# Strassen's block products for the second half of the last matrix product, in a kernel of attention, routed experts and a dense layer

## The chip, the core and the metric

The kernel runs on one core of a Trainium2 chip. The metric is device time in microseconds (us), from start to end of one execution. Smaller is better.

The core has a matrix engine (TensorE, PE in the profile; PEld is its loading of stationary weights), an elementwise engine (VectorE, DVE), an engine for functions and copies (ScalarE, ACT), GpSimd (POOL) and SyncE (SP), which here issues the transfers. Each engine works through its own list of instructions in order and waits on semaphores of the others.

## The reference, cut to what matters

```python
attn = softmax(mask(q @ k.T / 8))          # 4 x 8 heads, 576 positions, window of 64
x    = (attn @ v) as 2304 tokens x 512
logits = x @ phi                           # 8 experts x 4 slots
slot_out[e] = relu(slot_input[e] @ w1[e]) @ w2[e]
x = softmax(logits, over slots) @ slot_out
h = x @ w_in                               # 2304 x 512 by 512 x 2048
g = max(h, 0) + log1p(exp(-abs(h)))        # softplus
out = g @ w_out                            # 2304 x 2048 by 2048 x 512, float32
```

The change is in the last line. `w_in` and `w_out` arrive as 64-bit floats, and the kernel turns them into 32-bit ones itself.

## The kernel before, in words

Attention, routing and experts end at about 126.6 us of the trace. The change touches nothing ahead of that; what follows is the last phase.

**Units and groups.** The 2048 inner columns are 16 units of 128, the 2304 tokens 18 tiles of 128, in five groups (`GROUPS`) of 4, 4, 4, 3 and 3 tiles. For a group and a unit there is one item: TensorE makes `h` with the inner columns on the partitions (`do_h`, L933), ScalarE takes the softplus into `g` (`do_g`, L937).

**Split in two.** The matrix engine's fast 32-bit type keeps fewer digits than a float. So each operand is split: `gh` is `g` rounded to that type (`do_gh`, a cast at L838 on ScalarE or VectorE), `gl` is the rest `g - gh` (`do_gl`, L841 on VectorE); `w_out` is split likewise (tile `whl`, steps SH and SL). The product of a tile and a unit (step Y, `do_y`) is three matmuls into one PSUM bank of 512 columns: gh by high (L958), gh by low (L959), gl by high (L960). 18 tiles by 16 units by 3 are 864 of them.

**Turns.** `SLABS` cuts each group's units in three turns, since the weights arrive and are converted slowly (four elementwise steps for each of 32 chunks, `conv`, three of them on VectorE alone). A turn that ends leaves its sum in `part` (`do_o`: a copy after the first turn, an addition on VectorE after the second, L969; after the third an addition into `o` and the store, L975 and L976). One tile of the last group is taken in two halves of 256 columns in its last turn, so that its end comes sooner.

**Order.** Nothing is scheduled on the chip. `arrange` is a planner in the program that builds the kernel: from steps with assumed costs, dependences and due times it makes one list per engine. `TWEAKS` shifts due times by seeded random numbers. What it writes is a static order.

Of the kernel before, what the change touches and what calls it, by code (L numbers as in the profile page):

```python
# [44 lines left out]
DELAY = dict(E=0.2, Q=1.0)  # L45
# [87 lines left out]
def block_kernel(ctx: ExitStack, tc: tile.TileContext, qk, v, phi, w1, w2, w_in, w_out, out):
# [468 lines left out]
    with tc.manual_schedule():  # L602
# [168 lines left out]


        def conv(dst, src):
# [41 lines left out]
        parts_of = {2: (1,), 3: (2, 3), 4: (4, 5), 5: (6, 7)}  # L815

        def width(n):
            return 256 * len(parts_of[n])

        start = [sum(GROUPS[:g]) for g in range(len(GROUPS))]  # L820
        items = []
        for n in range(len(SLABS[0]) - 1):
            for g, nt in enumerate(GROUPS):
                a, b = SLABS[g][n:n + 2]
                for f in range(a, b):
                    cut = (0, 1, nt) if g == 0 and f == 0 else (0, nt)
                    items += [(g, f, f == a, f == b - 1, x, y) for x, y in zip(cut, cut[1:])]
        part, hl, st, y_t = {}, {}, {}, {}
# [133 lines left out]
        def do_o(e, i, j):
            g, f = items[i][:2]
            y, *more = y_t.pop((g, j))
            if f == SLABS[g][1] - 1:
                copy(e, part[g, j], y)
                return
            if f < 15:
                nc.vector.tensor_tensor(out=part[g, j], in0=y, in1=part[g, j], op=ALU.add)  # L969
                return  # L970
            ot = gp.tile([128, 512], F32, tag="o", name="o", bufs=3)
            t = start[g] + j
            for h, y in enumerate((y, *more)):
                c = slice(y.shape[1] * h, y.shape[1] * h + y.shape[1])
                nc.vector.tensor_tensor(out=ot[:, c], in0=y, in1=part[g, j][:, c], op=ALU.add)  # L975
                nc.sync.dma_start(out=out[128 * t:128 * t + 128, c], in_=ot[:, c])  # L976

        def do_r(e, *r):
# [12 lines left out]
        for h in range(2):
            step(("SO", h), dict(D=0.35), rel=L2_END + 0.42 * h - 0.3)
            step(("ST", h), dict(E=0.43), [("SO", h)])
            step(("SE", h), dict(A=0.26, D=0.33), [("ST", h)])
        for n, r in enumerate(raws):
            kind, j, u = r
            rest = [("C",) + raws[x] + (3,) for x in (n - 2 * NB, n - 2 * NB + 1) if n % 2 == 0 and x >= 0]
            step(("R",) + r, dict(Q=1.4), [("R",) + raws[n - 1]] + rest, rel=0.0 if n < NEARLY else 0.1 + 1.4 * NEARLY + 2.55 * NLAST)
            deps = [("R",) + r]
            if n:  # L1000
                deps.append(("C",) + raws[n - 1] + (0,))
            if n > 2:
                deps.append(("C",) + raws[n - 3] + (3,))
            deps += ([] if j < 3 else [("WD", 0, 1), ("WD", 1, 1)] if j == 3 else [("WA", (j - 3) // 2 + 2)]) if kind == "wi" else [("SL", 2 * j - 4 + u)]
            for k in range(4):
                costs = dict(D=0.335, A=0.62, P=1.0) if k == 0 else dict(D=(0.335, 0.6, 0.6)[k - 1])
                step(("C",) + r + (k,), costs, deps if k == 0 else [("C",) + r + (k - 1,)])
            if kind == "wo":
                m = 2 * j + u
                step(("SH", m), dict(A=0.58, D=0.42), [("C", "wo", j, u, 3), ("SH", m - 1)])  # L1010
                step(("SL", m), dict(P=1.25, D=0.69) if m < 2 else dict(D=0.69), [("SH", m)])
            elif j == 0:
                for h in range(2):
                    step(("WD", u, h), dict(E=0.45), [("C", "wi", 0, u, 3), ("SE", h), ("WD", u, h - 1)])
                step(("PC", u), dict(A=0.25, D=0.28), [("WD", u, 1)])
                step(("PS", u), dict(D=0.3), [("PC", u)])
            elif u == 1 and j % 2:
                n = (j + 3) // 2
                w = width(n) // 256
                step(("WA", n), dict(E=0.19 + 0.43 * w), [("C", "wi", x, y, 3) for x in parts_of[n] for y in range(2)] + [("PS", n - 1)])  # L1020
                step(("WQ", n), dict(A=0.26, D=0.33) if w == 1 else dict(A=0.59, D=0.69), [("WA", n), ("WB", n - 1)])
                step(("WL", n), dict(D=0.4 if w == 1 else 0.69), [("WQ", n)])
                step(("WB", n), dict(E=0.26 if w == 1 else 0.5), [("WL", n)])
# [77 lines left out]
```

## Time and profile before

| | |
|---|---|
| median of 3 runs | 361.4 us (361.08 to 362.69) |
| the profiled execution, its span from the first to the last instruction | 361.2 us |
| TensorE busy | 350.2 us (97%) |
| VectorE busy | 234.5 us (65%) |
| ScalarE busy | 155.6 us (43%) |
| last phase, 126.6 us to the end | 234.6 us |

The profiled execution is known by its span; 0.2 us lie between it and the median of the runs. Matmuls are pipelined: a record of one is longer than the distance to the next, and the distance from start to start is what one costs. The same holds for VectorE in a row of instructions that wait for nothing.

### The profile page before, as it was taken

To read this page: it belongs to the slowest core of one execution; us is meant where nothing else is said; L and a number is where in the kernel's file an instruction comes from. 1 tells how busy PE (TensorE), PEld (TensorE's weight loads), DVE (VectorE), ACT (ScalarE), POOL (GpSimd) and SP (SyncE) were. 2 spreads that over 40 slices of the span, in tenths; PEclk is the share of its full clock that TensorE was granted. 3 is DMA by queue.
4 is the path that set the end of the run, shared out by engine and by line. 5 is a ranking of instruction groups with operands and counts; after the bars stand their busy time and mean duration, and the time that the engine had idled before them with its cause. 6 is when DMAs were issued, how large, how long until landed. Compare 5 with 4: busy or idle time off the path is not lost.

```text
span 361.2 us, 7741 instructions
## 1 busy us (share of the span) xinstructions
PE 350.2 (97%) x2996; PEld 266.6 (74%) x2996; DVE 234.5 (65%) x717; ACT 155.6 (43%) x309; POOL 65.3 (18%) x93
## 2 busy tenths in 40 slices
PE   8999998999999999999999999999999999999995
PEld 6788776877434277877888878878888888888884
DVE  4677676874642299998999999954254263354632
ACT  1676665765410089876233656443034122122220
POOL 3997766771040000000000000000000000000000
PEclk9999999999999999999999999999999999999999
DMA  7999999999999964553053341000030020011102
GB/s 283 412 410 405 408 411 386 406 408 397 392 419 419 409 236 142 206 210 141 21 213 116 116 177 58 1 2 0 0 118 0 0 87 31 0 58 60 70 18 88
DMA packets 18180, 69.84 MB, mean 193 GB/s; under 512 B 2016, under 2 KB 2400, under 8 KB 14304
## 3 DMA queue, kind: packets, MB, share of 16 engines
q1 hardware_dynamic: 18000, 69.09, 49.1%
q8 instruction: 23, 0.38, 0.4%
q10 hardware_dynamic: 144, 0.26, 0.2%
q14 instruction: 13, 0.11, 0.1%
HBM read 64.63 MB, written 4.72 MB: 192 GB/s over the span
## 4 chain that ended last, share of the span: by engine, by line
PE 81%; DMA 13%; issue 1%; DVE 1%; POOL 1%; ACT 1%; SPq 0%; DVEq 0%; POOLq 0%; ACTq 0%
PE y_ps L959 19%; PE y_ps L958 19%; PE y_ps L960 18%; DMA w2t<-w_d 6%; PE x_ps L322 5%; DMA raw<-w_out_d 5%; PE pt_ps L304 5%; PE h_ps L933 5%; PE s_ps L277 4%; PE xt_ps L345 2%; DMA v_three<-v_d 2%; PE lt_ps L355 1%; PE wq_ps L900 1%; PE sl_ps L398 1%; POOL sm L295 1%
## 5 line engine op out<-in xcount | busy, mean ns | idle before, releaser
L959 PE MATMUL y_ps<-whl,gh 128*128 128x512 f32 (+1 forms) x295 | 115.6, 392 | 0.0
L958 PE MATMUL y_ps<-whl,gh 128*128 128x512 f32 (+1 forms) x295 | 114.9, 390 | 0.0
L960 PE MATMUL y_ps<-whl,gl 128*128 128x512 f32 (+1 forms) x295 | 114.5, 388 | 0.0
L937 ACT ACTIVATE g<-h_ps 128x512 f32<-128x512 f32 (+2 forms) x81 | 43.6, 553 | 105.7 <-PE h_ps L933 99.1
L958 PEld LDWEIGHTS y_ps<-whl,gh 128*128 128x128 f32 x295 | 55.4, 188 | 15.1 <-issue 2.5
L960 PEld LDWEIGHTS y_ps<-whl,gl 128*128 128x128 f32 x295 | 55.4, 188 | 12.4
L959 PEld LDWEIGHTS y_ps<-whl,gh 128*128 128x128 f32 x295 | 55.4, 188 | 11.4
L841 DVE TENSOR_TENSOR gl<-g,gh 128x512 fp32r<-128x512 f32 (+2 forms) x81 | 50.1, 628 | 3.8 <-ACT gh L838 1.6
L838 DVE CAST gh<-g 128x512 fp32r<-128x512 f32 (+1 forms) x48 | 19.1, 401 | 48.1 <-ACT g L937 47.3
L288 DVE CUSTOM_DVE_ANT_0 sm<-s_ps,cst_sb 128x128 f32<-128x128 f32 x144 | 32.1, 287 | 12.2 <-PE s_ps L277 11.5
L295 POOL TENSOR_TENSOR sm<-mx,sm 128x512 f32<-128x512 f32 x36 | 36.6, 1039 | 7.0 <-DVE mx L288 6.1
L933 PE MATMUL h_ps<-cT,wst 128*128 128x512 f32 (+2 forms) x81 | 28.4, 375 | 0.2 <-DVE wst L841 0.2
L298 ACT ACTIVATE sm<-sm 128x512 f32<-128x512 f32 x36 | 22.4, 635 | 12.0 <-POOL sm L295 11.9
L242 ACT COPY pt<-pt_ps 128x512 f32<-128x512 f32 x36 | 19.6, 588 | 11.8 <-PE pt_ps L304 11.6
L277 PE MATMUL s_ps<-qkb 64*64 64x128 f32 x576 | 21.3, 281 | 1.0 <-issue 0.9
L789 DVE SCALAR_TENSOR_TENSOR cv<-raw,cv 128x512 int32<-128x512 int32 x32 | 21.4, 686 | 0.1
L322 PE MATMUL x_ps<-vd,pt 128*64 128x65 f32 x288 | 21.1, 225 | 0.2
L975 DVE TENSOR_TENSOR o<-y_ps,part 128x512 f32<-128x512 f32 (+1 forms) x19 | 12.3, 661 | 13.3 <-PE y_ps L960 13.1
L322 PEld LDWEIGHTS x_ps<-vd,pt 128*64 128x64 f32 x288 | 18.4, 137 | 3.5 <-issue 2.5
L304 PE MATMUL pt_ps<-cst_sb,sm 128*128 128x128 f32 x144 | 19.7, 278 | 0.5 <-ACT sm L298 0.5
L838 ACT CAST gh<-g 128x512 fp32r<-128x512 f32 (+1 forms) x32 | 18.3, 573 | 3.5 <-PE y_ps L959 2.9
L277 PEld LDWEIGHTS s_ps<-qkb 64*64 64x64 f32 x576 | 16.5, 136 | 4.1 <-issue 3.6
(151 smaller groups left out, 413.0 us busy)
## 6 DMA issues: line engine op xcount, KB each, us to landing
w1t<-w_d SPq DMA_DIRECT2D x15, 1024.0 KB, 10.8
w2t<-w_d SPq DMA_DIRECT2D x13, 1024.0 KB, 11.5
qkb<-qk_d SPq DMA_DIRECT2D x17, 512.0 KB, 9.1
raw<-w_in_d SPq DMA_DIRECT2D x16, 512.0 KB, 4.1
raw<-w_out_d SPq DMA_DIRECT2D x16, 512.0 KB, 4.2
out_d<-o SPq DMA_DIRECT2D x17, 256.0 KB, 2.0
v_three<-v_d SPq DMA_DIRECT2D x10, 260.0 KB, 8.4
vt<-v_d SPq DMA_DIRECT2D x8, 260.0 KB, 8.5
```

The lines of the kernel that those rows point to most:

```text
L277: nc.tensor.matmul(s_ps[2 * t + a][64 * par:64 * par + 64, 128 * p:128 * p + 128], qkb[rows, b, 0, p, 64 * par:64 * par + 64], rhs, start= ...
L288: nc.vector.tensor_tensor_reduce(out=sm[:, p], in0=ps[:, 128 * p:128 * p + 128], in1=mask, scale=-0.125, scalar=3.0e38, op0=ALU.add, op1=A ...
L295: nc.gpsimd.tensor_tensor(out=sm_t[i], in0=mb, in1=sm_t[i], op=ALU.subtract)
L304: nc.tensor.transpose(ps[:, 128 * p:128 * p + 128], sm[:, p], ident)
L322: nc.tensor.matmul(x_ps[64 * par:64 * par + 64, a, 65 * p:65 * p + 65], pt[:, 128 * p + 64 * par:128 * p + 64 * par + 64], vt[:, 65 * h:65 ...
L838: (nc.scalar.copy if e == "A" else nc.vector.tensor_copy)(dst, src)
L841: eng[e].tensor_tensor(out=dst, in0=a, in1=b.bitcast(F32), op=ALU.subtract)
L933: nc.tensor.matmul(st["h", i], wst[:, 128 * f:128 * f + 128], cT[:, o:o + ncol(i)], start=True, stop=True)
L937: nc.scalar.activation(out=st["g", i], in_=st["h", i], func=AF.Softplus)
L958: nc.tensor.matmul(y, st["gh", i][:, ts], hi[:, c], start=first, stop=False)
L959: nc.tensor.matmul(y, st["gh", i][:, ts], lo[:, c], start=False, stop=False)
L960: nc.tensor.matmul(y, st["gl", i][:, ts], hi[:, c], start=False, stop=last)
```

## The change

Units 0 to 7 stay as they were, in two turns instead of three (`SLABS` has three numbers for a group). Groups are now 4, 4, 4, 4 and 2 tiles. Units 8 to 15 are taken in four pairs: for a group and a pair, `g` is a 2 by 2 matrix of blocks (two halves of the tokens by two units), and `w_out` one of two units by two halves of 256 columns. Strassen's method makes the 2 by 2 block product from seven block products in place of eight, each of a sum or difference of blocks. So:

- the sums of weights (steps TA, TB, TC into `txs`; TH, TL, TK, TM split them) are made once for each pair;
- the sums of tokens (XA, XB, XC, then HX, LX, HG, LG split them) are made for each group and pair, 20 times;
- each of the seven products (P, `do_p`) is three matmuls of 256 columns for every tile of half a group, summed over the four pairs in a PSUM bank of its own (banks 0 to 6; `h` uses bank 7);
- after the last pair each of the seven sums is copied out by ScalarE (MC, not in the last group) and added to or taken from up to four blocks of `part` by VectorE (M, `do_m`), which is stored from there.

The rounding casts `gh` and of the new splits stand on ScalarE alone. `TWEAKS` (47 entries) is replaced by another list (27 entries); with that and new costs the whole last phase has a new static order.

```diff
-GROUPS = (4, 4, 4, 3, 3)
-SLABS = ((0, 1, 5, 16), (0, 1, 6, 16), (0, 2, 7, 16), (0, 3, 8, 16), (0, 4, 9, 16))
+GROUPS = (4, 4, 4, 4, 2)
+NN = 8
+SLABS = ((0, 1, NN), (0, 2, NN), (0, 3, NN), (0, 4, NN), (0, 4, NN))
...
-ENGINES = dict(GL="D", GH="AD", SH="AD", SL="PD", WQ="AD", PC="A", O="AD", CE="AD", SO="D", SE="AD", C="AD")
+ENGINES = dict(GL="D", GH="A", SH="A", SL="PD", WQ="AD", PC="A", O="A", CE="AD", SO="D", SE="AD", C="AD", TH="A", TK="A", HX="A", HG="A")
...
-DELAY = dict(E=0.2, Q=1.0)
+DELAY = dict(E=0.2, Q=1.0, D=0.19, A=0.22)
...
+PRODUCTS = ((2, 5, 3), (3, 6, 2), (4, 0, 6), (5, 1, 5), (6, 4, 4), (0, 3, 1), (1, 2, 0))
...
+        def do_ta(e, j):
+            w = wt["pair", j]
+            eng[e].tensor_tensor(out=halves_of(txs[:, 0:512]), in0=two(w[:, 0:256], 512, 256), in1=two(w[:, 256:512], 512, 256), op=ALU.add)
...
+        def do_tl(e, j):
+            h, l = t_tiles(j)
+            sub(e, l[:, 0:1280], txs, h[:, 0:1280])
...
-            for h, y in enumerate(y_t[g, j]):
-                c = slice(y.shape[1] * h, y.shape[1] * h + y.shape[1])
-                nc.tensor.matmul(y, st["gh", i][:, ts], hi[:, c], start=first, stop=False)
-                nc.tensor.matmul(y, st["gh", i][:, ts], lo[:, c], start=False, stop=False)
-                nc.tensor.matmul(y, st["gl", i][:, ts], hi[:, c], start=False, stop=last)
+            nc.tensor.matmul(y, st["gh", i][:, ts], hi, start=first, stop=False)
+            nc.tensor.matmul(y, st["gh", i][:, ts], lo, start=False, stop=False)
+            nc.tensor.matmul(y, st["gl", i][:, ts], hi, start=False, stop=last)
...
+        def do_xa(e, s):
+            w, b = tokens(s), gbuf[s]
+            eng[e].tensor_tensor(out=xbuf(s)[:, 0:2 * w], in0=b[:, 0:2 * w], in1=b[:, 2 * w:4 * w], op=ALU.add)
+
+        def do_xb(e, s):
+            w, b = tokens(s), gbuf[s]
+            eng[e].tensor_tensor(out=halves_of(xbuf(s)[:, 2 * w:4 * w]), in0=halves_of(b[:, w:3 * w]), in1=two(b[:, 0:w], 3 * w, w), op=ALU.subtract)
...
+        def do_hx(e, s):
+            w = tokens(s)
+            copy(e, s_tile(s, 0)[:, 0:5 * w], xbuf(s)[:, 0:5 * w])
+
+        def do_lx(e, s):
+            w = tokens(s)
+            sub(e, s_tile(s, 1)[:, 0:5 * w], xbuf(s)[:, 0:5 * w], s_tile(s, 0)[:, 0:5 * w])
+
+        def do_p(e, s, i):
+            g, p = PAIRS[s]
+            b, x, y = PRODUCTS[i]
...
+            for n, (a, t) in enumerate(((0, hi), (0, lo), (1, hi))):
+                for j in range(nj):
+                    nc.tensor.matmul(
+                        ps[:, 256 * j:256 * j + 256], s_tile(s, a)[:, w * x + 128 * j:w * x + 128 * j + 128], t,
...
+        def do_mc(e, g, i):
+            w = 128 * GROUPS[g]
+            t = gp.tile([128, 512], F32, tag=("gh", "gl")[(7 * g + i) % 2], name="m")
+            nc.scalar.copy(t[:, 0:w], m_ps[g, i][:, 0:w])
...
+            def both(a, c, step, op):
+                x = v[:, a, :, 256 * c:256 * c + 256]
+                o = bass.AP(tensor=x.tensor, offset=x.offset, ap=[list(x.ap[0]), [step, 2], *(list(y) for y in x.ap[1:])])
+                mm = bass.AP(tensor=m.tensor, offset=m.offset, ap=[list(m.ap[0]), [0, 2], *(list(y) for y in m.ap[1:])])
+                nc.vector.tensor_tensor(out=o, in0=o, in1=mm, op=op)
...
+            if k == 5:
+                both(0, 1, 512 * nj, ALU.subtract)
+            elif k == 6:
+                both(0, 0, 512 * nj, ALU.add)
+            elif k == 0:
+                put(0, 1, ALU.add)
+                put(0, 0, ALU.subtract)
...
+            elif k == 3:
+                put(0, 0, ALU.add)
+                store(0)
```

**Place 1, TensorE at the start of the last phase, before.** `so_ps` and `wp_ps` turn the slots' outputs and `w_in` into the weights of `h`, `c_ps` transposes the routing weights, `warm_ps` is work without use.

```order
L855 MATMUL so_ps<-cst_sb,wit 128x128 x4
L889 MATMUL wp_ps<-wit,part 128x128 x4
L733 MATMUL c_ps<-identr,cc 128x128 x8
...
L889 MATMUL wp_ps<-wit,part 128x128 x2
L933 MATMUL h_ps<-cT,wst 128x512
L958 MATMUL y_ps<-whl,gh 128x512
L959 MATMUL y_ps<-whl,gh 128x512
L960 MATMUL y_ps<-whl,gl 128x512
L889 MATMUL wp_ps<-wit,part 128x128 x2
```

The same place now.

```order
L1032 MATMUL so_ps<-cst_sb,wit 128x128 x4
L1100 MATMUL wp_ps<-wit,part 128x128 x4
L919 MATMUL c_ps<-identr,cc 128x128 x12
...
L1144 MATMUL h_ps<-cT,wst 128x512
L1100 MATMUL wp_ps<-wit,part 128x128 x4
L1168 MATMUL y_ps<-whl,gh 128x512
L1169 MATMUL y_ps<-whl,gh 128x512
L1170 MATMUL y_ps<-whl,gl 128x512
```

All four `wp_ps` of the second unit now stand ahead of the first Y; two of them stood behind it.

**Place 2, VectorE in the second half of the last phase, before.** The casts and rests of `g`, and the final additions.

```order
L838 CAST gh<-g 128x512
L841 TENSOR_TENSOR gl<-g,gh 128x512
L975 TENSOR_TENSOR o<-y_ps,part 128x512
L838 CAST gh<-g 128x512
L841 TENSOR_TENSOR gl<-g,gh 128x512
L975 TENSOR_TENSOR o<-y_ps,part 128x512 x2
```

The same place now, one pair of a four-tile group and what stands between. `txs` and `cvx` hold the sums of tokens of alternate pairs, `shl` the split ones, `m` a copied product sum.

```order
L1213 TENSOR_TENSOR txs<-g_3548 128x512
L1217 TENSOR_TENSOR txs<-g_3548 128x512
L1221 TENSOR_TENSOR txs<-g_3548 128x256
L1273 TENSOR_TENSOR part<-part,m 128x4x256
L1012 TENSOR_TENSOR shl<-g_3548,shl 128x512
L1012 TENSOR_TENSOR shl<-txs,shl 128x1280
L1213 TENSOR_TENSOR cvx<-g_3599 128x512
L1221 TENSOR_TENSOR cvx<-g_3599 128x256
L1217 TENSOR_TENSOR cvx<-g_3599 128x512
L1273 TENSOR_TENSOR part<-part,m 128x4x256
```

The casts are gone from VectorE; sums of tokens, their rests and the additions of the block products have come.

**Place 3, VectorE at the very end, before.**

```order
L841 TENSOR_TENSOR gl<-g,gh 128x384 x2
L975 TENSOR_TENSOR o<-y_ps,part 128x512 x2
L975 TENSOR_TENSOR o<-y_ps,part 128x256 x2
```

And now (the 640 columns are the last pair's sums of tokens).

```order
L1012 TENSOR_TENSOR shl<-g_4481,shl 128x256
L1267 TENSOR_TENSOR part<-part,m 128x2x256
L1012 TENSOR_TENSOR shl<-cvx,shl 128x640
L1273 TENSOR_TENSOR part<-part,m_ps 128x2x256 x2
L1267 TENSOR_TENSOR part<-part,m_ps 128x256 x2
L1273 TENSOR_TENSOR part<-part,m_ps 128x2x256
L1267 TENSOR_TENSOR part<-part,m_ps 128x256 x4
```

Behind the last rest of tokens stand nine additions of the last group, where four final additions stood.

## Rows read from the trace of the kernel before

**Rows 1.** The page: busy time, share and instructions; busy tenths in 40 slices.
```profile
PE 350.2 (97%) x2996; PEld 266.6 (74%) x2996; DVE 234.5 (65%) x717; ACT 155.6 (43%) x309; POOL 65.3 (18%) x93
...
DVE  4677676874642299998999999954254263354632
```
**Rows 2.** Busy time by stretch: length, PE, PEld, DVE, ACT, POOL, clock, DMA.
```profile
126.60:132.60 6.00, 5.47 (x39) 4.70 (x40) 5.47 (x13) 5.45 (x13) 0.75 (x1) 1.00 0.77 281
132.60:235.00 102.40, 102.40 (x458) 80.82 (x457) 98.73 (x192) 59.52 (x115) 0.00 (x0) 1.00 0.35 127
235.00:356.80 121.80, 121.80 (x550) 98.51 (x548) 53.06 (x97) 30.66 (x56) 0.00 (x0) 1.00 0.09 34
356.80:361.20 4.40, 0.05 (x1) 0.00 (x0) 0.72 (x3) 0.00 (x0) 0.00 (x0) 1.00 0.39 138
```
**Rows 3.** The chain that ended last, shares of the span by engine.
```profile
PE 81%; DMA 13%; issue 1%; DVE 1%; POOL 1%; ACT 1%; SPq 0%; DVEq 0%; POOLq 0%; ACTq 0%
```
**Rows 4.** Groups by shape, Y's first matmul: count, busy us, mean ns, idle us.
```profile
L958 PE MATMUL y_ps<-whl,gh 128*128 128x512 f32 x281 | 111.0, 395 | 0.0
```
**Rows 5.** Timeline of PE, 512 columns: start us, length us, what.
```profile
252.98 0.40 PE L959 MATMUL y_ps<-whl,gh 128*128 128x512 f32 x1
...
255.78 0.40 PE L959 MATMUL y_ps<-whl,gh 128*128 128x512 f32 x1
```
**Rows 6.** Timeline of PE and its weight loads, 256 columns.
```profile
354.55 0.28 PE L958 MATMUL y_ps<-whl,gh 128*128 128x256 f32 x1
354.55 0.19 PEld L959 LDWEIGHTS y_ps<-whl,gh 128*128 128x128 f32 x1
354.67 0.29 PE L959 MATMUL y_ps<-whl,gh 128*128 128x256 f32 x1
...
355.27 0.40 PE L958 MATMUL y_ps<-whl,gh 128*128 128x512 f32 x1
```
**Rows 7.** Timeline of DVE while it is full.
```profile
180.14 0.42 DVE L784 TENSOR_SCALAR cv<-raw 128x512 f32<-128x512 f32 x1
180.47 0.68 DVE L841 TENSOR_TENSOR gl<-g,gh 128x512 fp32r<-128x512 f32 x1
181.08 0.68 DVE L790 SCALAR_TENSOR_TENSOR wit<-raw,cv 128x512 int32<-128x512 int32 x1
181.68 0.42 DVE L788 TENSOR_SCALAR cv<-cv 128x512 int32<-128x512 int32 x1
...
343.22 1.02 DVE L841 TENSOR_TENSOR gl<-g,gh 128x384 fp32r<-128x384 f32 x2
```
**Rows 8.** Groups by shape from 120 us on: DVE subtractions, ScalarE's casts.
```profile
L841 DVE TENSOR_TENSOR gl<-g,gh 128x512 fp32r<-128x512 f32 x47 | 32.0, 688 | 3.0 <-ACT gh L838 1.6
...
L841 DVE TENSOR_TENSOR gl<-g,gh 128x384 fp32r<-128x384 f32 x33 | 17.8, 554 | 0.8
...
L838 ACT CAST gh<-g 128x512 fp32r<-128x512 f32 x17 | 10.6, 624 | 2.9 <-PE y_ps L959 2.6
```
**Rows 9.** Groups by shape, DVE, operands repeated or in pieces, and one plain.
```profile
L337 DVE TENSOR_TENSOR xn<-x_ps,ri 128x512 f32<-128x512 f32 x18 | 12.4, 691 | 0.5
...
L712 DVE TENSOR_TENSOR cc<-lnat,cc 128x128 fp32r<-128x128 f32 x4 | 1.5, 372 | 0.1
...
L789 DVE SCALAR_TENSOR_TENSOR cv<-raw,cv 128x512 int32<-128x512 int32 x32 | 21.4, 686 | 0.1
...
L841 DVE TENSOR_TENSOR gl<-g,gh 128x128 fp32r<-128x128 f32 x1 | 0.3, 278 | 0.0
```
**Rows 10.** Timeline of PE around the first Y.
```profile
132.62 0.39 PE L958 MATMUL y_ps<-whl,gh 128*128 128x512 f32 x1
...
133.31 0.61 PE L889 MATMUL wp_ps<-wit,part 128*128 128x128 f32 x4
```
**Rows 11.** Timeline of the end.
```profile
356.17 1.35 DVE L975 TENSOR_TENSOR o<-y_ps,part 128x512 f32<-128x512 f32 x3 [0.73 <-PE y_ps L960]
...
356.57 0.28 PE L960 MATMUL y_ps<-whl,gl 128*128 128x256 f32 x1
```

More of the change, by code (lines that the diff above doesn't have):

```diff
@@ L24 @@
 XTB, XNB = 5, 6
[L25 to L26 removed]
+GROUPS = (4, 4, 4, 4, 2)
+NN = 8
+SLABS = ((0, 1, NN), (0, 2, NN), (0, 3, NN), (0, 4, NN), (0, 4, NN))
+NP = (16 - NN) // 2
+START = [sum(GROUPS[:g]) for g in range(len(GROUPS))]
+PARTS_OF = {2: (1,), 3: (2, 3), 4: (4, 5), 5: (6, 7)}
 NX, NB = 5, 3
@@ L129, in arrange @@
     return sorted(order, key=lambda x: x[0])
+RAWS = [("wi", 0, 0), ("wo", 0, 0), ("wi", 0, 1), ("wo", 0, 1)]
+RAWS += [(k, j, u) for j in range(1, 8) for k in ("wi", "wo") for u in range(2)]
+ITEMS = []
+for _n in range(len(SLABS[0]) - 1):
+    for _g, _nt in enumerate(GROUPS):
+        _a, _b = SLABS[_g][_n:_n + 2]
+        for _f in range(_a, _b):
+            _cut = (0, 1, _nt) if _g == 0 and _f == 0 else (0, _nt)
+            ITEMS += [(_g, _f, _f == _a, _f == _b - 1, x, y) for x, y in zip(_cut, _cut[1:])]
@@ L791, in conv @@
             ]
-        raws = [("wi", 0, 0), ("wo", 0, 0), ("wi", 0, 1), ("wo", 0, 1)]
-        raws += [(k, j, u) for j in range(1, 8) for k in ("wi", "wo") for u in range(2)]
-        for r in raws[:NEARLY]:
+        for r in RAWS[:NEARLY]:
             load_raw(*r)
@@ L814, in block_kernel @@
         wq = gp.tile([128, 1024], F32R, tag="wq", name="wq", bufs=1)
[L815 to L828, printed above, removed]
+        txs = gp.tile([128, 1280], F32, tag="tx", name="txs", bufs=1)
+        part, hl, st, y_t, t_hl, s_hl, m_ps = {}, {}, {}, {}, {}, {}, {}
+        parts = []
         for n, x in enumerate((g, j) for g, nt in enumerate(GROUPS) for j in range(nt)):
             if n % 4 == 0:
-                pt4 = wpx.tile([128, 2048], F32, tag="w", name="part")
-            part[x] = pt4[:, 512 * (n % 4):512 * (n % 4) + 512]
-        soT = pt4[:, 1024:1536]
+                parts.append(wpx.tile([128, 2048], F32, tag="w", name="part"))
+            part[x] = parts[-1][:, 512 * (n % 4):512 * (n % 4) + 512]
+        soT = parts[-1][:, 1024:1536]
         eng = dict(A=nc.scalar, D=nc.vector, P=nc.gpsimd)
@@ L881, in do_sl, with t_tiles, do_tb, do_tc @@
             sub(e, l, wt.pop(("wo", j, u)), h)
+        def t_tiles(j):
+            if j not in t_hl:
+                t_hl[j] = [wpa.tile([128, 2048], F32R, tag="w", name=n) for n in ("thi", "tlo")]
+            return t_hl[j]
+        def do_ta(e, j):
+            w = wt["pair", j]
+            eng[e].tensor_tensor(out=halves_of(txs[:, 0:512]), in0=two(w[:, 0:256], 512, 256), in1=two(w[:, 256:512], 512, 256), op=ALU.add)
+        def do_tb(e, j):
+            w = wt["pair", j]
+            eng[e].tensor_tensor(out=txs[:, 512:1024], in0=w[:, 512:1024], in1=w[:, 0:512], op=ALU.subtract)
+        def do_tc(e, j):
+            w = wt["pair", j]
+            eng[e].tensor_tensor(out=txs[:, 1024:1280], in0=w[:, 0:256], in1=w[:, 768:1024], op=ALU.add)
+        def do_tk(e, j):
+            copy(e, halves_of(t_tiles(j)[0][:, 1280:1792]), two(wt["pair", j][:, 0:256], 768, 256))
+        def do_tm(e, j):
+            h, l = (halves_of(x[:, 1280:1792]) for x in t_tiles(j))
+            sub(e, l, two(wt["pair", j][:, 0:256], 768, 256), h)
+        def do_th(e, j):
+            copy(e, t_tiles(j)[0][:, 0:1280], txs)
+        def do_tl(e, j):
+            h, l = t_tiles(j)
+            sub(e, l[:, 0:1280], txs, h[:, 0:1280])
         def do_wd(e, u, h):
@@ L929, in do_h @@
         def do_h(e, i):
-            g, f, first, last, ta, tb = items[i]
-            o = 128 * (start[g] + ta)
-            st["h", i] = bank(hb[i], "h_ps")[:, 0:ncol(i)]
+            g, f, first, last, ta, tb = ITEMS[i]
+            o = 128 * (START[g] + ta)
+            st["h", i] = bank(HBANK[i], "h_ps")[:, 0:ncol(i)]
             nc.tensor.matmul(st["h", i], wst[:, 128 * f:128 * f + 128], cT[:, o:o + ncol(i)], start=True, stop=True)
@@ L971, in do_o, with do_h2 @@
[L971 to L976, printed above, removed]
+        def do_h2(e, s, u):
+            g, p = PAIRS[s]
+            n, f = 128 * GROUPS[g], NN + 2 * p + u
+            o = 128 * START[g]
+            st["h2", s, u] = bank(7, "h_ps")[:, 0:n]
+            nc.tensor.matmul(st["h2", s, u], wst[:, 128 * f:128 * f + 128], cT[:, o:o + n], start=True, stop=True)
@@ new lines, in block_kernel, with s_tile, tokens @@
+        gbuf, n_s = {}, [0]
+        def s_tile(s, h):
+            z = s - 4 * NP
+            r = s if z < 0 else s - z % 2
+            if (r, h) not in s_hl:
+                k = n_s[0]
+                n_s[0] += 1
+                s_hl[r, h] = mp.tile([128, 3072], F32R, tag="wit", name="shl") if k % 4 == 3 else wpb.tile([128, 2048], F32R, tag="w", name="shl")
+            return s_hl[r, h] if z < 0 else s_hl[r, h][:, 896 * (z % 2):896 * (z % 2) + 896]
+        def tokens(s):
+            return 64 * GROUPS[PAIRS[s][0]]
@@ new lines, in do_g2, with xbuf @@
+        def do_g2(e, s, u):
+            n = 2 * tokens(s)
+            if u == 0:
+                gbuf[s] = gp.tile([128, 1024], F32, tag="wq", name="g2", bufs=1) if s % 3 == 1 else tp.tile([128, 1024], F32, tag="wo", name="g2", bufs=2)
+            nc.scalar.activation(out=gbuf[s][:, n * u:n * u + n], in_=st.pop(("h2", s, u)), func=AF.Softplus)
+        def xbuf(s):
+            return txs if s > 1 and s % 2 == 0 else cvx
+        def do_xa(e, s):
+            w, b = tokens(s), gbuf[s]
+            eng[e].tensor_tensor(out=xbuf(s)[:, 0:2 * w], in0=b[:, 0:2 * w], in1=b[:, 2 * w:4 * w], op=ALU.add)
@@ new lines, in do_xb, with do_xc, do_hg @@
+        def do_xb(e, s):
+            w, b = tokens(s), gbuf[s]
+            eng[e].tensor_tensor(out=halves_of(xbuf(s)[:, 2 * w:4 * w]), in0=halves_of(b[:, w:3 * w]), in1=two(b[:, 0:w], 3 * w, w), op=ALU.subtract)
+        def do_xc(e, s):
+            w, b = tokens(s), gbuf[s]
+            eng[e].tensor_tensor(out=xbuf(s)[:, 4 * w:5 * w], in0=b[:, 0:w], in1=b[:, 3 * w:4 * w], op=ALU.add)
+        def do_hg(e, s):
+            w, b = tokens(s), gbuf[s]
+            copy(e, halves_of(s_tile(s, 0)[:, 5 * w:7 * w]), two(b[:, 0:w], 3 * w, w))
@@ new lines, in do_lg @@
+        def do_lg(e, s):
+            w, b = tokens(s), gbuf[s]
+            sub(e, halves_of(s_tile(s, 1)[:, 5 * w:7 * w]), two(b[:, 0:w], 3 * w, w), halves_of(s_tile(s, 0)[:, 5 * w:7 * w]))
+        def do_hx(e, s):
[5 more added lines that the diff above has]
+        def do_p(e, s, i):
+            g, p = PAIRS[s]
+            b, x, y = PRODUCTS[i]
+            w, nj = tokens(s), GROUPS[g] // 2
+            if p == 0:
+                m_ps[g, i] = bank(b, "m_ps")
+            ps = m_ps[g, i]
+            hi, lo = (t[:, 256 * y:256 * y + 256] for t in t_hl[NN // 2 + p])
+            for n, (a, t) in enumerate(((0, hi), (0, lo), (1, hi))):
+                for j in range(nj):
+                    nc.tensor.matmul(
+                        ps[:, 256 * j:256 * j + 256], s_tile(s, a)[:, w * x + 128 * j:w * x + 128 * j + 128], t,
+                        start=p == 0 and n == 0 and j == 0, stop=p == NP - 1 and n == 2, skip_group_check=True,
+                    )
@@ L991, in block_kernel @@
[L991 to L1023, printed above, removed]
-                step(("PC", n), dict(A=0.26, D=0.33) if w == 1 else dict(A=0.59, D=0.69), [("WB", n)])
-                step(("PS", n), dict(D=0.33 if w == 1 else 0.69), [("PC", n)])
```

258 lines of the change are left out of this document (205 added, 53 removed).

## The prediction

> **What bounds the kernel now.** I read the page's busy times first, then the stretches of the last phase, the chain, and then single distances. TensorE is busy for 97% of the span, VectorE for 65%, and VectorE's digits are 9 in the slices from about 126 to 235 us and half of that behind [rows 1]. The stretches sharpen it: from 132.6 us to 356.8 TensorE has no idle time at all at a clock of 1.00; VectorE is busy 98.73 of 102.40 us up to 235, but 53.06 of 121.80 after it, ScalarE 30.66 [rows 2]. The chain that ended last agrees, with 81% on TensorE [rows 3]. So the last phase lasts as long as TensorE's matmuls, and what matters of a matmul is not the 395 ns of its record [rows 4] but the distance to the next. For 512 columns that is (255.78 - 252.98) / 12 = 0.2333 us [rows 5], for 256 columns (355.27 - 354.55) / 6 = 0.120 us [rows 6]. The kernel before runs in both shapes, so the new products' price stands in its trace.
>
> **Products removed and added.** Units 8 to 15 cost 18 tiles x 8 units x 3 = 432 matmuls of 512 columns, 432 x 0.2333 = 100.8 us. The new order has 756 of 256 columns (7 products x 3 x 9 half-tiles x 4 pairs), 756 x 0.120 = 90.7 us. Net -10.1. Seven eighths would be 88.2; the missing 2.5 us are the shorter matmul's worse distance. Bounds: 88.2, if 256 columns cost half of 512, and, since the run of six is short, 0.125 each, 94.5. I take the measured distance. The split of one tile in halves (42 of 256 for 21 of 512) goes: 21 x 0.2333 - 42 x 0.120, -0.1. The `h` products cover the same columns in other pieces: 0.
>
> One price could overturn this, the stationary weights. A load is recorded with 0.19 us, more than 0.120. But the load that began at 354.55 belongs to the matmul that began at 354.67, beside the one of 354.55 that runs until 354.83 [rows 6]: loads lie beside matmuls and beside each other, and do not set the distance. The Trainium skill (TensorE: Matmul & The Clock Gate, Part 3, "The mechanism") says that a weight load overlaps a running matmul only where the two use different row groups; here all use the whole array, so by that rule every load would stand alone and the change, with 324 more matmuls, would lose. The trace does not agree: 0.120 us is less than its load alone.
>
> **The start.** Two more `wp_ps` stand ahead of the first Y. In the trace the pair of them lies in a row of four matmuls of 0.61 us [rows 10], so about 0.3 us; they also wait for a conversion on VectorE. They are not new work, only early, so below nothing (-0.2) and up to +0.7 are possible, the latter if that conversion comes late. I take +0.3.
>
> **VectorE.** Its instructions too cost their distance: 0.60 for 512 columns of two operands, 0.33 for one operand, 1.02 - 0.554 = 0.466 for 384 columns (the last row merges two, and one has 554 ns) [rows 7, 8]. From 512 and 384 a straight line gives estimates of 0.19 for 128, 0.33 for 256, 0.74 for 640, 1.14 for 1024 and 1.41 for 1280. Second half by the counts of the order: sums of tokens 32 x 0.60 + 24 x 0.33 + 4 x 0.19 = 27.9; rests 16 x (0.60 + 1.41) + 4 x (0.33 + 0.74) = 36.4; additions of block products (24 + 3) x 0.60 + 12 x 1.14 + 6 x 0.33 = 31.9. Together 96.2 us, against 90.7 + 8.4 (40 `h` of two shapes, 18,432 columns at 0.2333 for 512) = 99.1 us of TensorE. Before, VectorE was busy 44% of that time [rows 2]. So the change spends nearly all of the slack that the trace shows, and TensorE stays the longer by 2.9 us.
>
> Can VectorE run that full? From 132.6 to 235 it had 98.73 / 102.40 = 96.4% and TensorE did not wait [rows 2]. At 96.4%, 96.2 us of work need 99.8, 0.7 us more than TensorE's 99.1; since its work does not come evenly I take +1.0. It will fall near the end: the two-tile group gives TensorE 4 x 7 x 3 x 0.120 + 8 x 0.12 = 11.0 us, while VectorE has 4 x (0.33 + 0.33 + 0.19 + 0.33 + 0.74) = 7.7 for it and the nine additions of the group ahead, 3 x 1.14 + 6 x 0.60 = 7.0, still to do. The bounds of this term are 0 and, if each of the 145 instructions cost its recorded 0.688 instead of 0.60 [rows 7, 8], 145 x 0.087 = 12.6 us.
>
> Are the new forms dearer? They read and write in pieces of 256 columns or repeat an operand. A multiplication with a repeated operand in pieces of 64 has 691 ns, a conversion that reads every second word 686, the plain subtraction 688 [rows 8, 9]: no extra. One row speaks otherwise: a subtraction that writes pieces of 32 has 372 ns where a plain one of that size has 278 [rows 9]. GpSimd worked on the same tile then; I go by the others, 0, and keep the 94 ns for a rival.
>
> In the plain turns VectorE gets the sums of weights, 8 x 0.60 + 4 x 0.33 + 4 x (0.60 + 1.41) = 14.2 us, and the casts leave it. Conversions 32 x 1.53 + 12 x 0.33 = 52.9, rests of g 21.9, additions 10.8, weight rests 4.8 and some 5 for the weights of `h` make 109.6 us, beside TensorE's 100.8 + 8.4 + some 8 for the weights of `h` and the start, 117: 93%, under what it bore before. Cost 0; if that cover failed, it would be late first for the fourth pair's weights, which can be split only when units 4 to 7 are done.
>
> ScalarE gets casts and copies: in the second half 32 softplus, 28 copies and 16 casts of 512 columns, at most 0.62 each by the row of the cast, 16 casts of 1280, at most 2.5 times that, and 16 small ones: 76 x 0.62 + 16 x 1.55 + some 7 = 79 of 99 us [rows 8]. It was idle for 91 of 121.8 [rows 2]. Cost 0 as long as VectorE hides its rounding: a pair's rest waits for ScalarE's cast, and what stands between on VectorE is an addition or the next pair's sums.
>
> **The end.** Before, the last matmul began at 356.57, VectorE was done at 356.17 + 1.35 = 357.52, and the span ended 3.7 us after that, with the last store [rows 11]. Now nine additions follow the last rest of tokens, 3 x 0.60 + 6 x 0.33 = 3.8 us. TensorE needs that rest for five products of 3 x 0.120, 1.8 us, plus about 0.2 for the handover. VectorE ends some 1.8 us after the last matmul begins, where it was 0.95: +0.8 (bounds 0.5 and 1.5). The last store is one of 256 KB for one of 128; I keep the 3.7.
>
> **Sum.** -10.1 - 0.1 + 0.3 + 1.0 + 0.8 = -8.1. The profiled span 361.2 becomes 353.1, and with the 0.2 us between span and median, 353.3 us.
>
> **Rival A, VectorE becomes the bound.** Half of its 145 instructions in the second half cannot overlap the next one, because they wait for ScalarE or for a tile: 96.2 + 6.3 = 102.5 us, 3.4 more than TensorE, and at 96.4% it is 7.2. In place of the +1.0: 361.4 - 9.1 + (3.4 to 7.2) = 355.7 to 359.5, about 357.6. For it: the two engines lie within 3%, and only two or three pairs are buffered. Against: the stretch up to 235 us.
>
> **Rival S, slower: pieces slow VectorE.** The price is the 94 ns for 128 columns, 0.73 ns a column, on what is read or written in pieces: differences of tokens and their rests 18,432 columns, additions 27,648, so 46,080 x 0.73 = 33.8 us at full price. It decides from 12.0 us on, where the whole gain of 9.1 and the 2.9 of slack are gone: at a good third of the price. At half, 16.9, VectorE needs 113.1 us and the time is 361.4 - 9.1 + 14.0 = 366.3. Against it stand the three forms without extra, one of them with smaller pieces.
>
> **Rival W, weights set the pace.** If in a long run loads went 0.188 us apart, the products took 756 x 0.188 = 142.1 us: 361.4 - 9.1 + 51.4 = 403.7. The run of six speaks against it [rows 6]. By the skill's rule above, each matmul more would also bring its load of 0.19 us into the open, 324 of them 61.6 us, and the time would be 361.4 - 9.1 + 61.6 = 413.9; it shares the 0.01.
>
> **That the products are not saved** is out: the order has 756 block matmuls and 432 of Y where 864 products stood.
>
> **How the numbers follow.** Forecast 0.74 (its own range 351 to 356), A 0.14, S 0.07, W 0.01, and 0.04 for a better end than any term allows for (no stall, and products nearer to half price: 349 to 351). Range: the low end takes 1.0 of stall and about 1.3 of the product bound away, 351.0; the high end goes to the middle of A, 358.0; left out are S, W, half of A and the last 0.04, some 0.19. A measurement of this kernel can tell 0.5%, 1.8 us. Faster than 359.6: forecast, the better end and 0.11 of A (its slow end can pass its 359.5 a little), 0.89. Within: 0.03 of A and 0.01 of S, 0.04. Slower: the rest of S and W, 0.07.
>
> **What would show it.** Right: block matmuls 0.120 us apart over hundreds of them, at clock 1.00; the first Y within 0.7 us of where it was; VectorE at 95% or more in the second half with TensorE's idle time under 1.5 us, most of it in the last 15 us; VectorE's last addition about 1.8 us behind the start of the last matmul. Wrong: weight loads in a distance of 0.188; additions in pieces recorded well over 0.69 for 512 columns or 1.24 for 1024; VectorE waiting for ScalarE's casts while TensorE waits for a rest; or an idle TensorE between the plain turns and the first products.

## The result, and the profile after

The changed kernel takes 351.87 us (351.86 to 352.93, 4 runs), the kernel before 361.38 us (361.08 to 362.69, 4 runs). The ratio is 0.9734, with a 95% interval of 0.9710 to 0.9759. Forecast were 353.3 us and a range of 351.0 to 358.0.

First the page of the changed kernel: busy time and VectorE's 40 slices, as in [rows 1].

```profile
PE 338.5 (97%) x3298; PEld 273.4 (78%) x3298; DVE 286.6 (82%) x767; ACT 205.7 (59%) x385; POOL 65.2 (19%) x93
...
DVE  5687776875452289999999996988988999999996
```

VectorE went from 65% to 82%. From about 123 us on its digits are 8 or 9 but for one 6 (at 210 to 219 us) and the last slice; before, they fell to half from 235 us on. The stretches of the last phase, columns as in [rows 2]:

```profile
132.60:240.00 107.40, 107.40 (x481) 83.40 (x480) 100.49 (x182) 71.99 (x132) 0.00 (x0) 1.00 0.35 119
...
246.00:334.00 88.00, 88.00 (x706) 86.56 (x705) 84.44 (x118) 59.26 (x95) 0.00 (x0) 1.00 0.10 37
334.00:346.20 12.20, 11.11 (x92) 10.88 (x91) 11.99 (x26) 4.51 (x10) 0.00 (x0) 1.00 0.24 87
346.20:350.20 4.00, 0.00 (x0) 0.00 (x0) 0.72 (x2) 0.00 (x0) 0.00 (x0) 0.84 0.38 133
```

TensorE is without idle time until its last matmul, at a clock of 1.00, and VectorE beside it is at 96% and then 98%. Now the places at which the phase can be cut: the end of the experts' product before (first fence) and after, the first Y, and the end.

```profile
125.48 1.07 PE L679 MATMUL l_end<-w2t,hTz 128*32 128x256 f32 x16 [0.54 <-DMA w2t<-w_d]
```

```profile
123.91 1.05 PE L865 MATMUL l_end<-w2t,hTz 128*32 128x256 f32 x16
...
130.86 0.48 PE L1168 MATMUL y_ps<-whl,gh 128*128 128x512 f32 x1
...
344.83 0.28 PE L1249 MATMUL m_ps<-thi,shl 128*128 128x256 f32 x1
345.32 1.60 DVE L1267 TENSOR_TENSOR part<-part,m_ps 128x256 f32<-128x256 f32 x4
```

With [rows 10, 11] and the spans of 361.2 and 350.2 us that gives

| stretch | before | after | difference | forecast |
|---|---|---|---|---|
| span's start to the end of `l_end`, unchanged code | 126.55 | 124.96 | -1.6 | 0 |
| to the first Y | 6.07 | 5.90 | -0.2 | +0.3 |
| first Y to the start of the last matmul | 223.95 | 213.97 | -10.0 | -9.2 |
| to the end of VectorE's last addition | 0.95 | 2.09 | +1.1 | +0.8 |
| to the end of the span | 3.68 | 3.28 | -0.4 | 0 |

The phase lost 9.4 us, as the medians say (9.5). The 1.6 us ahead of it are taken as no part of the change: the code there is the same, and the profiled execution of before was a long one. In later runs of that kernel with both numbers known, spans of 360.0 and 361.0 us went with times of 361.66 and 362.68, so 1.7 us lie around a span, not 0.2. By that estimate the one with a span of 361.2 took about 362.9, some 1.5 us above the median.

### The profile page after: what moved, and what is told of

The parts are those of the page before. It is cut to its first block, busy times and chain, and to the rows that moved or that the text cites. A ratio compares the mean times of both kernels' runs of the same rounds, so it can differ in the third digit from the quotient of the medians.

```text
span 350.2 us, 8448 instructions
## 1 busy us (share of the span) xinstructions
PE 338.5 (97%) x3298; PEld 273.4 (78%) x3298; DVE 286.6 (82%) x767; ACT 205.7 (59%) x385; POOL 65.2 (19%) x93
## 4 chain that ended last, share of the span: by engine, by line
PE 87%; DVE 5%; issue 2%; DMA 1%; ACT 1%; POOL 1%; SPq 0%; DVEq 0%; POOLq 0%; ACTq 0%
PE m_ps L1249 21%; PE y_ps L1168 10%; PE y_ps L1169 10%; PE y_ps L1170 10%; PE x_ps L508 5%; PE pt_ps L490 5%; PE s_ps L463 4%; PE l_ps L815 4%; PE l_ps L865 4%; PE xt_ps L531 2%; PE h_ps L1144 2%; PE h_ps L1186 2%; DVE part L1267 1%; DMA v_three<-v_d 1%; PE lt_ps L541 1%
## 5 line engine op out<-in xcount | busy, mean ns | idle before, releaser
L1249 PE MATMUL m_ps<-thi,shl 128*128 128x256 f32 x504 | 87.7, 283 | 0.0
L1249 PEld LDWEIGHTS m_ps<-thi,shl 128*128 128x128 f32 x504 | 74.8, 190 | 1.4
L1168 PE MATMUL y_ps<-whl,gh 128*128 128x512 f32 x144 | 57.3, 398 | 0.0
L1169 PE MATMUL y_ps<-whl,gh 128*128 128x512 f32 x144 | 57.2, 397 | 0.0
L1170 PE MATMUL y_ps<-whl,gl 128*128 128x512 f32 x144 | 56.8, 395 | 0.0
L1249 PE MATMUL m_ps<-tlo,shl 128*128 128x256 f32 x252 | 53.0, 283 | 0.0
L1249 PEld LDWEIGHTS m_ps<-tlo,shl 128*128 128x128 f32 x252 | 40.0, 190 | 0.0
L1168 PEld LDWEIGHTS y_ps<-whl,gh 128*128 128x128 f32 x144 | 27.0, 188 | 9.4 <-issue 1.7
L1170 PEld LDWEIGHTS y_ps<-whl,gl 128*128 128x128 f32 x144 | 27.0, 188 | 7.0 <-DVE gl L1012 0.6
L1169 PEld LDWEIGHTS y_ps<-whl,gh 128*128 128x128 f32 x144 | 27.1, 188 | 5.8
L1009 ACT CAST gh<-g 128x512 fp32r<-128x512 f32 (+2 forms) x40 | 23.0, 581 | 4.6 <-PE y_ps L1169 4.1
L1012 DVE TENSOR_TENSOR gl<-g,gh 128x512 fp32r<-128x512 f32 (+3 forms) x41 | 25.2, 621 | 0.5 <-ACT gh L1009 0.3
```

The lines of the kernel that those rows point to most:

```text
L1009: (nc.scalar.copy if e == "A" else nc.vector.tensor_copy)(dst, src)
L1012: eng[e].tensor_tensor(out=dst, in0=a, in1=b.bitcast(F32), op=ALU.subtract)
L1168: nc.tensor.matmul(y, st["gh", i][:, ts], hi, start=first, stop=False)
L1169: nc.tensor.matmul(y, st["gh", i][:, ts], lo, start=False, stop=False)
L1170: nc.tensor.matmul(y, st["gl", i][:, ts], hi, start=False, stop=last)
L1249: nc.tensor.matmul(ps[:, 256 * j:256 * j + 256], s_tile(s, a)[:, w * x + 128 * j:w * x + 128 * j + 128], t, start=p == 0 and n == 0 and j ...
```

## The experiments

All edits are to the changed kernel; its time is 351.87. The table gives medians and the ratio to the kernel before, measured beside each.

| run | us | ratio, 95% interval | against 351.87 |
|---|---|---|---|
| VectorE +3.0 us | 354.38 | 0.9807 (0.9779 to 0.9835) | +2.5 |
| VectorE +6.1 us | 357.85 | 0.9901 (0.9871 to 0.9932) | +6.0 |
| VectorE +10.9 us | 361.57 | 1.0001 (0.9986 to 1.0016) | +9.7 |
| TensorE -30.2 us | 348.51 | 0.9648 (0.9620 to 0.9676) | -3.4 |
| VectorE -5.5 us | 351.01 | 0.9708 (0.9693 to 0.9722) | -0.9 |
| casts to VectorE, +6.1 us | 356.70 | 0.9872 (0.9850 to 0.9893) | +4.8 |
| planner without shifts | 354.41 | 0.9799 (0.9782 to 0.9817) | +2.5 |
| sums to GpSimd at the end | 353.32 | 0.9771 (0.9754 to 0.9787) | +1.5 |
| TensorE +8.4 us | 359.98 | 0.9957 (0.9938 to 0.9976) | +8.1 |
| last store in two | 352.11 | 0.9732 (0.9712 to 0.9752) | +0.2 |

**How much VectorE can bear.** Three runs repeat instructions of VectorE with the same values, so that the order of all other work stays.

```diff
         def do_xc(e, s):
             w, b = tokens(s), gbuf[s]
-            eng[e].tensor_tensor(out=xbuf(s)[:, 4 * w:5 * w], ...)
+            for _ in range(1 + s % 2):     # second run: range(2); third: do_lg twice
+                eng[e].tensor_tensor(out=xbuf(s)[:, 4 * w:5 * w], ...)
```

> In every second pair of the second half VectorE makes one of its sums of tokens (128x256, in the two-tile group 128x128) a second time, with the same values: 10 instructions, 8 x 0.33 + 2 x 0.20 = 3.0 us more for VectorE, nothing else changed. Theory (VectorE has some 2.9 us less to do than TensorE in the second half, and TensorE never waits for it): the 3.0 us use up that slack, time 351.9 to 353.0, TensorE's last matmul later by at most 1. Rival A (VectorE is the bound already): +3.0, 354.9. Rival F (VectorE is far from the bound, its instructions overlap): 351.9.

> The same sum is made twice in every pair: 16 x 0.33 + 4 x 0.20 = 6.1 us more for VectorE. Theory (slack 2.9 us): +3.2, about 355. Rival A (bound already): +6.1, 358. Rival F (far from the bound): 351.9.

> In every pair VectorE makes one rest (128x512, in the two-tile group 128x256) twice, with the same values: 16 x 0.60 + 4 x 0.33 = 10.9 us more for VectorE. Theory (slack 2.9 us): +8.0, about 360, with TensorE idle for about that long in the second half. Rival A: +10.9, 362.8. Rival F: 351.9 to 353.

Measured +2.5, +6.0 and +9.7: from the first microsecond nearly all of it comes on the time. The theory's slack of 2.9 us is not there, and the rival that VectorE is a bound already came closer. The traces say the same: from the first Y to the start of the last matmul the three runs take 216.2, 219.1 and 223.3 us, 2.2, 5.1 and 9.4 more than the 214.0 of the changed kernel. In the first run:

```profile
130.79 0.48 PE L1168 MATMUL y_ps<-whl,gh 128*128 128x512 f32 x1
...
347.00 0.28 PE L1250 MATMUL m_ps<-thi,shl 128*128 128x256 f32 x1
```

The third run shows the ways it takes: the waits of TensorE's weight loads from 240 us on (us, times, longest), and then the longest of them in order of time.

```profile
PEld m_ps L1250 <- DVE shl L1012: 4.9, 9, 1.1
PEld h_ps L1186 <- ACT g L1206: 3.2, 4, 1.6
PEld m_ps L1250 <- ACT m L1258: 0.7, 1, 0.7
```

```profile
331.12 0.42 DVE L1221 TENSOR_TENSOR cvx<-g 128x256 f32<-128x256 f32 x1
...
331.57 1.26 ACT L1009 CAST shl<-cvx 128x1280 fp32r<-128x1280 f32 x1 [2.36 <-DVE cvx L1221]
...
332.74 0.38 ACT L1206 ACTIVATE g<-h_ps 128x256 f32<-128x256 f32 x1
...
333.17 0.19 PEld L1186 LDWEIGHTS h_ps<-cT,wst 128*128 128x128 f32 x1 [1.64 <-ACT g L1206]
```

Most of it, 4.9 us in nine waits, is a rest of VectorE that TensorE needs at once and that comes late. The longest single wait goes a longer way: VectorE's last sum ends late, ScalarE is idle for it 2.36 us before its cast of 1280 columns, the softplus queued behind that cast is late, and TensorE's next `h` has no free bank for 1.64 us.

**The same from TensorE's side.**

```diff
-            for n, (a, t) in enumerate(((0, hi), (0, lo), (1, hi))):
+            for n, (a, t) in ((0, (0, hi)), (2, (1, hi))):          # fourth run
...
-            nc.tensor.matmul(st["h2", s, u], wst[...], cT[...], start=True, stop=True)
+            for _ in range(2):                                       # ninth run
+                nc.tensor.matmul(st["h2", s, u], wst[...], cT[...], start=True, stop=True)
```

> The block products leave out the matmul by the low part of the weights: 252 of 756 matmuls go, 30.2 us of TensorE's second half, and nothing of VectorE or ScalarE (the computation is changed by that part). Theory (VectorE is only 2.9 us below TensorE): VectorE takes over as the bound, time falls by 2 to 5 us, to 347 to 350, and TensorE is idle for about 26 us. Rival F (VectorE far from the bound): it falls by most of 30, to 323 to 330.

> Each of the 40 h products of the second half is made twice into the same bank, with the same values: 32 x 0.2333 + 8 x 0.12 = 8.4 us more for TensorE, nothing for VectorE. Theory (the engines are level, and TensorE has no idle time to give): nearly all of it comes on the time, less the 0.65 us that it waits now and some of VectorE's tail: +6.5 to 8, 358.4 to 360. Rival A (VectorE alone is the bound of the second half, TensorE only keeps pace with it): TensorE could take some of it in, as VectorE waits 4.0 us for ScalarE there, +2 to 5, 354 to 357.

Without 252 matmuls (the products then lack that part) the time falls by 3.4 us, not by 30; with 8.4 us more it rises by 8.1. So neither engine alone is the bound: each, made longer, moves the end, and neither, made shorter, moves it far. In the fourth run VectorE is as full as ever while TensorE waits (stretch from 246 to 341 us):

```profile
246.00:341.00 95.00, 77.37 (x544) 70.19 (x542) 93.91 (x139) 62.86 (x104) 0.00 (x0) 0.98 0.12 44
```

TensorE's granted clock fell once in this run, after a stretch with many waits: from 330 to 334 us it was busy for 2.31 of 4.00 us, and from 336 to 338 us the clock was 0.50, its lower level of 1.2 GHz. Matmuls then began 0.213 us apart. VectorE was full beside it, so no cost of that to the end shows.

```profile
330.00:334.00 4.00, 2.31 (x20) 2.11 (x19) 4.00 (x9) 2.59 (x7) 0.00 (x0) 1.00 0.01 4
336.00:338.00 2.00, 2.00 (x11) 2.00 (x11) 2.00 (x6) 0.72 (x1) 0.00 (x0) 0.50 0.00 0
```

In the ninth it is the other way round, VectorE 96.24 of 107.00 us:

```profile
246.00:353.00 107.00, 107.00 (x836) 104.10 (x835) 96.24 (x140) 65.95 (x105) 0.00 (x0) 1.00 0.11 40
```

**Less for VectorE.** The second of two additions is left out for two products in every group, so the sums are not complete.

```diff
             elif k == 0:
                 put(0, 1, ALU.add)
-                put(0, 0, ALU.subtract)
...
             elif k == 1:
                 put(1, 0, ALU.add)
-                put(1, 1, ALU.subtract)
```

> Eight additions of 512 columns and two of 256 are left out of the block products' sums (the second one of two products in every group), 8 x 0.60 + 2 x 0.33 = 5.5 us less for VectorE, nothing else (the computation is changed by that part). Theory now (the two engines are level: TensorE waits 0.65 us in the second half, and behind its last matmul VectorE has 2.1 us left): only those waits and part of the tail can go, time falls by 0.6 to 1.5 us, to 350.4 to 351.3. Rival A (VectorE is the bound of the whole second half, and what is taken from it comes off the time as what was added came on): it falls by about 5, to 347.

351.01, 0.9 us less; by the times alone the two intervals overlap. The trace says where it is: the additions end 344.45 + 1.23 - 344.60 = 1.08 us after the last matmul began, where it was 2.09.

```profile
344.45 1.23 DVE L1267 TENSOR_TENSOR part<-part,m_ps 128x256 f32<-128x256 f32 x3
...
344.60 0.28 PE L1249 MATMUL m_ps<-thi,shl 128*128 128x256 f32 x1
```

As expected: VectorE's work is worth its tail and no more, since TensorE has nothing else to give back.

**A part undone: casts on VectorE again.** `do_hg` copies with VectorE in place of ScalarE.

> The casts of the unsummed blocks (16 of 512 columns, 4 of 256) go back from ScalarE to VectorE: 16 x 0.33 + 4 x 0.20 = 6.1 us more for VectorE, 9.9 us or more less for ScalarE. Theory (level engines): as with a sum made twice, +5 to 6, about 357.5. Rival B (what cost time in that run was that ScalarE's casts came later, not VectorE's time): less than +2, since ScalarE is relieved, 352 to 354.

+4.8, between the two, nearer to the theory: ScalarE's relief does not make up for VectorE's time.

**The order alone.** `TWEAKS = ()`.

> The planner's list of random shifts is empty; steps, costs and dependences stay, the order of the last phase is the planner's own. Theory (two engines at 97 to 99% leave no room for an uneven order): some us slower, 354 to 358. Rival (the order hardly matters, sums of work do): within 1 us of 351.9.

+2.5. In its trace (an execution of 353.47 us) the first Y comes 0.7 us later behind `l_end`, from there to the last matmul it takes 215.6 us for 214.0, and the tail is 0.6 shorter. With two engines this full the order is worth about a quarter of the whole gain.

**Two tries at the end.** GpSimd makes the first sum in the two-tile group and the last store is cut in two; then the store alone.

```diff
-            eng[e].tensor_tensor(out=xbuf(s)[:, 0:2 * w], ...)
+            eng["P" if s >= 4 * NP else e].tensor_tensor(out=xbuf(s)[:, 0:2 * w], ...)   # eighth run only
...
             elif k == 3:
+                if g == len(GROUPS) - 1:
+                    store(0, 256)
                 put(0, 0, ALU.add)
-                store(0)
+                store(0, 0, 256 if g == len(GROUPS) - 1 else 512)
```

> In the two-tile group the first sum of tokens (4 of 128x256) is made by GpSimd, which has nothing else to do there, and the last store is cut in two so that half of it starts before the last addition. VectorE has 4 x 0.33 = 1.3 us less in the last 25 us. Theory (VectorE's rest of work sets the end): 0.7 to 1.3 us faster, about 351. Rival C (GpSimd needs about twice as long for a sum, half of the 1039 ns of a 512-column one, and delays the casts that need all three sums): no gain or up to 1 us slower.

> The last store alone is cut in two, so that half of it starts before the last addition of 256 columns; nothing else changed. Theory (VectorE's rest of work and then a transfer of about 3.3 us, whatever its size, end the span): within 0.3 us of 351.9. Rival (the size of the last store matters): 0.3 to 0.8 us faster.

The store does nothing: +0.2, within the interval, and the span ends 3.28 us after the last addition, as in the changed kernel. GpSimd brings no gain and probably a loss: the interval of its ratio lies just above that of the run with the store alone, and only just touches that of the changed kernel. First GpSimd's four sums, then what VectorE did at the same time:

```profile
324.31 1.27 POOL L1213 TENSOR_TENSOR txs<-g 128x256 f32<-128x256 f32 x1 [193.96 <-ACT g L1206]
328.26 0.80 POOL L1213 TENSOR_TENSOR cvx<-g 128x256 f32<-128x256 f32 x1 [2.69 <-ACT g L1206]
333.63 1.86 POOL L1213 TENSOR_TENSOR txs<-g 128x256 f32<-128x256 f32 x1 [4.57 <-DVE shl L1012]
339.33 0.98 POOL L1213 TENSOR_TENSOR cvx<-g 128x256 f32<-128x256 f32 x1 [3.83 <-ACT shl L1009]
```

```profile
324.35 0.42 DVE L1221 TENSOR_TENSOR cvx<-g 128x256 f32<-128x256 f32 x1
...
324.97 1.15 DVE L1012 TENSOR_TENSOR shl<-g,shl 128x512 fp32r<-128x512 f32 x1
...
328.39 1.22 DVE L1267 TENSOR_TENSOR part<-part,m 128x512 f32<-128x512 f32 x1
...
334.82 1.76 DVE L1273 TENSOR_TENSOR part<-part,m 128x1024 f32<-128x1024 f32 x1
...
339.63 0.96 DVE L1012 TENSOR_TENSOR shl<-g,shl 128x256 fp32r<-128x256 f32 x1
```

Beside each of GpSimd's sums one instruction of VectorE is longer than in the changed kernel: 1.15 us for 0.69, 1.22 for 0.69, 1.76 for 1.22 and 0.96 for 0.42. Together VectorE loses 2.1 us, more than the 1.3 that GpSimd took from it, and from the first Y to the last matmul it takes 0.65 us more. The Trainium skill has a rule for it (SBUF — State Buffer, "Who interferes with whom"): a VectorE instruction with two inputs from SBUF contends with a GpSimd instruction that reads SBUF. The trace agrees for these four; others beside the same sums kept their length, as the 0.42 us at 324.35. Why it met just these four stays open.

## Why the prediction was right, and which terms were off

**Products: right.** 756 block matmuls lie 0.120 us apart over the whole half: here 18 from 248.11 to 250.27.

```profile
248.11 0.64 PE L1249 MATMUL m_ps<-thi,shl 128*128 128x256 f32 x4
...
250.27 0.40 PE L1249 MATMUL m_ps<-thi,shl 128*128 128x256 f32 x2
```

The run of six in [rows 6] was enough to price them. Rival W is out: loads are still recorded with 0.19 us, and the merged row below shows two of them in 0.31, 0.12 apart.

```profile
250.74 0.19 PEld L1249 LDWEIGHTS m_ps<-thi,shl 128*128 128x128 f32 x1
...
250.86 0.31 PEld L1249 LDWEIGHTS m_ps<-tlo,shl 128*128 128x128 f32 x2
```

**Operands in pieces: right, rival S out.** Groups by shape of the changed kernel: an addition in pieces has 686 ns, a plain rest 688 before; 1024 and 1280 columns have 1221 and 1488, where the straight line plus the 0.087 us by which a record is longer gave 1.23 and 1.50.

```profile
L1267 DVE TENSOR_TENSOR part<-part,m 128x512 f32<-128x512 f32 x24 | 15.6, 686 | 0.2
L1273 DVE TENSOR_TENSOR part<-part,m 128x1024 f32<-128x1024 f32 x12 | 14.6, 1221 | 1.9 <-ACT m L1257 1.8
L1012 DVE TENSOR_TENSOR shl<-cvx,shl 128x1280 fp32r<-128x1280 f32 x9 | 13.4, 1488 | 0.5 <-ACT shl L1009 0.5
```

**VectorE's stall: +1.0 forecast, 0.2 found.** Taking 0.120 and 0.2333 us a matmul off the distances of the second half, 0.16 us are left in all, at 333.9 and here, where two matmuls of 0.24 fill 0.33:

```profile
338.27 0.49 PE L1249 MATMUL m_ps<-thi,shl 128*128 128x256 f32 x2
338.60 0.28 PE L1249 MATMUL m_ps<-tlo,shl 128*128 128x256 f32 x1
```

Both are in the two-tile group, as forecast; this 0.8 is the largest part of the gap. (Two expectations name 0.65 us for it, which was misread.)

That the stall stayed so small was in part luck: the prediction put a price on how full VectorE is, not on the order, and with the planner's own order the same work makes TensorE wait 1.6 us.

What the text said of the slack was wrong in the other direction. "TensorE stays the longer by 2.9 us" is true of the sums (VectorE is busy 95.33 of 99.00 us from 246 to 345), but the idle time is this, VectorE's waits in that stretch (us, times, longest; the 0.8 ended just ahead of it), and then the two parts of the stretch:

```profile
DVE part L1273 <- ACT m L1257: 1.8, 2, 1.5
DVE shl L1012 <- ACT shl L1009: 1.1, 2, 0.6
DVE cvx L1213 <- ACT g L1206: 0.8, 1, 0.8
DVE cvx L1217 <- ACT g L1206: 0.3, 1, 0.3
```

```profile
246.00:287.00 41.00, 41.00 (x326) 40.13 (x325) 37.56 (x52) 26.74 (x41) 0.00 (x0) 1.00 0.06 21
287.00:344.83 57.83, 57.83 (x472) 57.23 (x471) 57.60 (x89) 37.03 (x64) 0.00 (x0) 1.00 0.16 59
```

3.4 us of it lie ahead of 287 us and 0.2 behind, where VectorE is busy for 57.60 of 57.83 us. That is 99.6%, so the 96.4% from which the prediction sized the stall was no limit; and work added there cannot use what was idle before: 3.0 us more cost 2.5. TensorE's matmuls end 2.2, 5.1 and 9.4 us later in the first three runs, counted from the first Y, so what VectorE had free was about 0.8 us of the first 3.0. Rival A had the mechanism and the wrong side of it: the kernel stands on the edge, not beyond it.

**The start: +0.3 forecast, -0.2 found.** The two early `wp_ps` cost nothing that can be told from the rest. **The end: +0.8 forecast, +1.1 found** for VectorE's tail: the nine additions behind the last rest take from 342.67 to 346.92 us, 4.25 us for the 3.8 of the forecast. And 0.4 the other way behind it, which the store's size does not explain; that stays open.

**The base.** 0.2 us between the profiled span and the median was no property of an execution: the profile was of a slower one, and 1.7 us lie around a span. The forecast took a difference from the median, so this did not move it. The gap of 1.4 us, 353.3 to 351.87, is 0.8 of stall, 0.5 of start and 0.4 behind the last addition, with 0.3 the other way in the tail.

## What to carry to other kernels

Price a matmul by its distance to the next in the same shape, and look for a short run of the new shape in the old trace: six were enough here. Idle time is not slack: before trusting 3% of it on a second engine, repeat an instruction there and see whether the time moves. When two engines are level, only work taken from both, or the tail behind the last of them, is still worth anything.

## What was not expected of the hardware

A GpSimd sum of 256 columns took 0.80 to 1.86 us beside VectorE, and beside each of the four such sums one VectorE instruction of 256 to 1024 columns took about half a microsecond longer, while others beside them did not.
